# Another order of steps in the first phase and in all periods of a fused attention and feed-forward kernel

## The chip, the cores and the metric

The kernel runs on one core of one Trainium2 chip. The metric is the device time of one execution in microseconds (us); where several executions are shown, their median. All times below are in us unless marked ns. The engines are named as in the profile: PE is TensorE (PEld its weight loads), DVE VectorE, ACT ScalarE, POOL GpSimd and SP SyncE, which here only issues DMAs.

## What is computed

Nyström attention over 8 batches of 8 heads (sequence 576, head size 64, 32 landmarks), and on its result a multiplicative feed-forward layer without a nonlinearity.

```python
q_lm = q.reshape(B, H, m, S // m, D).mean(axis=3)      # 32 landmarks
k_lm = k.reshape(B, H, m, S // m, D).mean(axis=3)
A  = softmax(scale * q @ k_lm.T)
Bm = softmax(scale * q_lm @ k_lm.T)
C  = softmax(scale * q_lm @ k.T)
Z = Bm.T / (norm1(Bm) * norminf(Bm) + 1e-06)
for _ in range(6):
    Z = 2 * Z - Z @ Bm @ Z
x = (A @ Z @ C @ v) as rows of 512                     # 4608 rows
out = ((x @ w1) * (x @ w2)) @ w3 @ w_out               # 512 -> 1024 -> 1024 -> 512
```

Inputs and output are float32; the products run in float16 or float32.

## The kernel before

The kernel is one program whose engines each work through their instructions in the order in which the program issues them; what an engine needs from another it waits for. The order is written out by hand, in five strings of short names (lines 45 to 58 of the profile's line numbers), and `run` issues the steps one after the other. START is issued once, after a fixed beginning that loads weights and starts to fold w3 and w_out into one matrix. Then come eight periods, one for each batch b: FIRST for b = 0, ODD and EVEN in turn for b = 1 to 6, LAST for b = 7. A period b does the attention of batch b+1 up to the matrix g that stands for everything between the normalised A and the feed-forward layer, the first scores C of batch b+2, the two up projections of batch b, and down projections of pairs of batches. START does the whole attention of batch 0 and the scores C of batch 1.

The names, with the engines that each step uses:

- `f`: one product of the fold of w3 and w_out, three PE matmuls of 512 columns; eleven of those in the strings first turn a block of w3 (four PE transposes, one ACT and one DVE copy). `w`: a load of w3 (SP). `x`: turning batch 0's q or k on PE. `v`: batch 0's v (SP).
- `t`: one of four DMA transposes of a batch's q and k (SP). `p`: one of four loads of a batch's v (a tiny ACT copy, then SP). `s`: landmark sums of q or of k, four POOL additions, and between them two POOL-issued loads of the q and k of a later batch. `h`: one of four halves of the landmarks, an ACT copy (tile far) and a POOL addition (tiles qbd for q, lm for k).
- `C0 C1`: scores against all keys (12 PE matmuls each), ACT exponential, three POOL sums (tiles t, es). `S0 S1`: their denominators, two PE matmuls of one column each. `V0 V1`: product with v, 48 small PE matmuls, then an ACT copy into sz.
- `A0 A1`: scores of all queries against the landmarks, PE, then an ACT exponential. `D`: their denominators (PE); `J0 J1 J2` invert them in thirds, `X` splits the result (DVE). `M0 M1`: normalise A (PE, then DVE into ahat).
- `B`, `T`, `N`, `P`, `R`: the landmark matrix Bm (PE, ACT, DVE, POOL), its transpose (DVE, POOL), its norms (DVE), two scaled copies (POOL), the first residual (PE, DVE, POOL).
- `I0` to `I5`: the six steps of the inverse, 16 matmuls of 32x32 each on PE, then a DVE sum (tz) and copy (sz) on which the next step waits. `Z`: closes it (PE, ACT, DVE into zt).
- `G0` to `G3`: zt times w1 and w2, 16 matmuls of 512 columns each, evicted by ACT (even) or DVE (odd) into g.
- `u`: half of a pair of up projections: four PE matmuls; the first of a pair is copied by ACT, the second is multiplied with that copy by DVE. `d` and `db`: half of a down projection, four PE matmuls of 512 columns; the second half ends with an ACT eviction (o_sb) and the output stores on SP. With `d` a new item takes the one bank of tile acc, with `db` one of the three double banks of tile big, which u, I, C, A, G and M share.

On PE most steps use the whole array (u, d, f, C, M, S). A, B, R and G use parts of 64x32, D and V of 128x32, I of 32x32, Z of 128x64; these are called tiled steps, and the shapes tile shapes.

Of the kernel before, what the change touches and what calls it, by code (L numbers as in the profile page):

```python
# [13 lines left out]
B = 8  # L14
H = 8
S = 576
D = 64
# [14 lines left out]
def kernel(  # L32
# [9 lines left out]
    out: bass.AP,  # L42
):
    nc = tc.nc
    START = ("w v x x s f f f f f x x w f f h h s f f w t t f f f f f C0 f f h f h f w t t "
             "S0 C1 B f T f f N V0 f S1 A1 f A0 R D P V1 f J0 I0 p f J1 J2 I1 f f f f f f f "
             "X s I2 p f I3 f f f p I4 f M0 I5 h f s t Z M1 f h f G0 G1 t h f f G2 p h G3 f "
             "f C0 C1 f f t ")
    FIRST = ("u u p S0 u t u B p p u A1 V0 A0 T N u P R u u f s S1 u u D V1 I0 u J1 I1 f J0 "
             "s I2 u h u h J2 I3 u X I4 u u M0 I5 d M1 Z h d t G0 h G1 d p C0 t t G2 C1 G3 "  # L50
             "db ")
    EVEN = ("u S0 u t B u u T V0 A1 u N u u R db u p S1 db A0 V1 p p s u I0 t P D u J0 u I1 "
            "J1 d u I2 db J2 X u I3 u u s I4 M0 I5 h h M1 u Z db h G0 t h G1 db C0 d p G2 t "
            "G3 C1 db ")
    ODD = ("p u S0 t u B A1 p T u p V0 N d R u u S1 s u u d u A0 V1 u I0 D J2 u u I1 J0 d "
           "s I2 P h u u I3 h J1 u u I4 t h d I5 u db X t t d d Z M0 d M1 G0 p G1 C0 d G2 "
           "G3 C1 h db ")
    LAST = ("u u d u u u d u u u d u u u u d u u u u d d db d db db db db db d ")
    consts = ctx.enter_context(tc.tile_pool(name="consts", bufs=1))
    wpool = ctx.enter_context(tc.tile_pool(name="wpool", bufs=1))  # L60
    pin = ctx.enter_context(tc.tile_pool(name="pin", bufs=2))
# [477 lines left out]
    def steps(g, n=1):  # L539
        for _ in range(n):  # L540
            next(g, None)
# [71 lines left out]
    def run(names):  # L613
        for t in names.split():
            if t[0] in queues:
                next(queues[t[0]], None)
            elif t == "f":
                steps(fd)
            elif t[0] == "d":
                piece(acc if t == "d" else lambda: big()[:, 0, :])  # L620
            else:
                n = done[t] = done.get(t, -1) + 1
                while len(atts) <= n and n < B:
                    atts.append(attention(sts[len(atts)]))
                if n < B:
                    atts[n][t[0]](*([int(t[1])] if t[1:] else []))
# [4 lines left out]
    with tc.tile_pool(name="pf", bufs=2) as pf:  # L631
# [50 lines left out]
        steps(fd, 8)  # L682
        run(START)
    pabs = [ctx.enter_context(tc.tile_pool(name="pab0", bufs=1))]
    for b in range(B):
        if b % 2 == 0:
            ab = pabs[b // 2 % len(pabs)].tile([128, 8, 2 * S], FP16, name="ab%d" % (b // 2 % 2))
        sts[b]["ab"], sts[b]["t0"] = ab, S * (b % 2)
        run(FIRST if b == 0 else LAST if b == B - 1 else (EVEN, ODD)[b % 2])
        if b == 0:  # L690
# [32 lines left out]
```

## Time and profile before

| | |
|---|---|
| median of 4 runs | 273.48 us (272.36 to 274.88) |
| the profiled execution: time, span | 272.36 us, 270.6 us |
| granted TensorE clock | 0.998 |
| PE busy | 262.5 us, 97% |
| POOL, DVE, ACT busy | 171.5, 150.6, 143.5 us |
| START begins at (start of its first x) | 18.84 us |
| FIRST begins at (first u) | 67.09 us |
| first ODD, first EVEN, second ODD, second EVEN begin at | 91.92, 118.63, 143.80, 170.18 us |
| last PE work ends at | 266.4 us |

The profile is of one execution. The span goes from its first to its last instruction; the time of the execution has 1.8 us around that. A row of the timeline gives the start and the duration of a group of instructions; on PE the duration holds the time in the pipeline as well, so that the next row begins before the last one ends. What a step costs PE is therefore read from the start of one row to the start of the next.

### The profile page before, as it was taken

The page shows a single profiled execution, that of the slowest core. Times are in us where ns is not written, and L with a number is a line of the kernel's source. Part 1 is how long each engine was busy: PE and PEld are TensorE (multiplying, and loading weights), DVE is VectorE, ACT ScalarE, POOL GpSimd, SP SyncE. Part 2 cuts the span into 40 slices and gives each one's busy share as a digit, 9 for nine tenths or more (in the row PEclk, how much of TensorE's full clock was granted, in tenths as well). Part 3 has the DMA queues.
Part 4 walks back from the last instruction along what each step waited for, and adds up shares of the span by engine and source line. Part 5 has one row for each costly group of instructions (what it writes and reads, how often), then busy time and mean ns, then how long its engine had stood idle before and what let it go on. Part 6 is the DMA issues. An engine that isn't in the chain of part 4 may idle for free.

```text
span 270.6 us, 9335 instructions
## 1 busy us (share of the span) xinstructions
PE 262.5 (97%) x3876; PEld 148.1 (55%) x3876; DVE 150.6 (56%) x380; ACT 143.5 (53%) x276; POOL 171.5 (63%) x237
## 2 busy tenths in 40 slices
PE   8999999999999999999999999999999999999993
PEld 3565555554554565466546654655465556545742
DVE  5643235453567558554866574749466566674420
ACT  4644454246634954385367645844855475435531
POOL 6818971499699879666986994699869545000000
PEclk9999999999999999999999999999999999999999
DMA  6999999999967999998999999989993141113144
GB/s 206 370 241 264 225 249 188 201 219 147 190 137 106 187 184 220 195 186 155 200 168 233 207 169 162 198 131 238 162 257 99 39 125 42 41 42 80 39 111 121
DMA packets 62138, 45.56 MB, mean 168 GB/s; under 512 B 35600, under 2 KB 54288, under 8 KB 62096
## 3 DMA queue, kind: packets, MB, share of 16 engines
q1 hardware_dynamic: 47488, 32.22, 57.0%
q0 software_dynamic: 13824, 11.54, 29.7%
q10 hardware_dynamic: 784, 1.21, 1.4%
q8 instruction: 30, 0.49, 0.8%
q14 instruction: 12, 0.10, 0.1%
HBM read 38.80 MB, written 9.44 MB: 178 GB/s over the span
## 4 chain that ended last, share of the span: by engine, by line
PE 77%; POOL 7%; DMA 5%; SPq 3%; DVE 3%; issue 1%; ACT 1%; DVEq 0%; POOLq 0%
PE big L430 23%; PE acc L471 15%; PE big L471 8%; DMA qkT<-qkn 5%; PE big L379 5%; PE big L413 4%; PE acc L510 4%; PE small L323 4%; SPq L124 3%; PE big L665 2%; PE small L510 2%; DVE ab L436 2%; PE big L230 2%; PE big L497 1%; PE big L364 1%
## 5 line engine op out<-in xcount | busy, mean ns | idle before, releaser
L430 PE MATMUL big<-ahat,gt 128*128 128x288 f16 x512 | 76.1, 286 | 0.4
L436 DVE TENSOR_TENSOR ab<-a_sb,big 128x576 f16<-128x576 f16 x64 | 48.2, 753 | 27.0 <-ACT a_sb L434 15.0
L434 ACT CAST a_sb<-big 128x576 f16<-128x576 f32 x64 | 40.8, 638 | 35.4 <-PE big L430 35.2
L430 PEld LDWEIGHTS <-gt 128*128 128x128 f16 x512 | 46.9, 99 | 19.5
L471 PE MATMUL acc<-w,ab 128*128 128x512 f16 x184 | 47.3, 380 | 0.0
L471 PEld LDWEIGHTS <-ab 128*128 128x128 f16 x280 | 24.3, 99 | 25.9 <-issue 3.2
L510 PE MATMUL acc<-wsp,w3t 128*128 128x512 f16 x144 | 35.4, 380 | 0.0
L194 POOL TENSOR_TENSOR tr<-qkT 128x768 f32<-128x768 f16 x16 | 26.3, 1641 | 7.9 <-DMA qkT<-qkn 7.5
L419 DVE TENSOR_SCALAR gt<-big 128x1024 f16<-128x1024 f32 x16 | 19.6, 1225 | 18.0 <-PE big L413 18.0
L510 PEld LDWEIGHTS <-w3t 128*128 128x128 f16 x192 | 17.9, 98 | 18.0 <-issue 0.8
L195 POOL TENSOR_TENSOR tr<-tr,qkT 128x768 f32<-128x768 f32 x16 | 26.3, 1643 | 1.3
L238 POOL TENSOR_TENSOR t<-ect 96x384 f32<-96x384 f32 x16 | 15.9, 997 | 15.9 <-ACT ect L234 13.8
L471 PE MATMUL big<-w,ab 128*128 128x512 f16 x96 | 23.4, 380 | 0.0
L475 ACT ACTIVATE o_sb<-acc 128x512 f32<-128x512 f32 x23 | 13.7, 596 | 14.0 <-PE acc L471 13.8
L503 DVE SCALAR_TENSOR_TENSOR w3t<-big,w3t 128x512 f16<-128x512 f32 x16 | 11.0, 690 | 18.0 <-ACT w3t L502 18.0
L379 PE MATMUL big<-sz,tz 32*32 32x96 f32 (+1 forms) x768 | 18.9, 248 | 1.1 <-DVE sz L386 0.7
L417 ACT ACTIVATE gt<-big 128x1024 f16<-128x1024 f32 x16 | 16.4, 1023 | 6.3 <-PE big L413 6.3
L384 DVE TENSOR_TENSOR tz<-big,eye 128x64 f32<-128x64 f32 x40 | 8.8, 221 | 15.8 <-PE big L379 15.1
L213 ACT COPY far<-o 64x256 f32<-64x256 f32 x32 | 12.9, 403 | 8.4 <-POOL o L199 7.6
L413 PE MATMUL big<-wup,zt 64*32 64x512 f16 x512 | 17.1, 379 | 0.0
L379 PEld LDWEIGHTS big<-sz,tz 32*32 32x32 f32 x768 | 8.9, 102 | 14.5 <-issue 10.7
L502 ACT ACTIVATE w3t<-big 128x512 f16<-128x512 f32 x16 | 9.5, 596 | 11.0 <-PE big L497 10.9
(104 smaller groups left out, 374.1 us busy)
## 6 DMA issues: line engine op xcount, KB each, us to landing
vt<-in_v_dram SPq DMA_DIRECT2D x28, 288.0 KB, 4.9
out_dram<-o_sb SPq DMA_DIRECT2D x23, 192.0 KB, 2.8
qkn<-in_q_dram POOLq DMA_DIRECT2D x12, 288.0 KB, 5.7
qkn<-in_k_dram POOLq DMA_DIRECT2D x12, 288.0 KB, 6.1
w3f<-in_moe_w_dram SPq DMA_DIRECT2D x6, 512.0 KB, 8.3
out_dram<-o_sb SPq DMA_DIRECT2D x24, 128.0 KB, 2.8
wup<-in_moe_w_dram POOLq DMA_DIRECT2D x4, 512.0 KB, 31.6
out_dram<-o_sb SPq DMA_DIRECT2D x23, 64.0 KB, 2.8
```

Of the source, the lines that this page charges most:

```text
L194: nc.gpsimd.tensor_tensor(out=tr, in0=x[:, :, 0, :], in1=x[:, :, 1, :], op=ALU.add)
L195: nc.gpsimd.tensor_tensor(out=tr, in0=tr, in1=x[:, :, 2, :], op=ALU.add)
L238: nc.gpsimd.tensor_tensor(out=t3[0:NP], in0=e[:, :, 0:3, :], in1=e[:, :, 3:6, :], op=ALU.add)
L379: nc.tensor.matmul(psI[32 * t:32 * t + 32, qd, o:96], tz[sl, qd, :], sz[sl, qd, o:96], start=True, stop=True, tile_position=(32 * h, 32 * t))
L413: nc.tensor.matmul(psG[32 * h:32 * h + 32, qd, :], zt[rs, i, h, :], wup[rs, h, w, fs], start=(i == 0), stop=(i == 1), tile_position=(64 * ...
L417: nc.scalar.activation(out=g[:, :, w, fs], in_=psG, func=AXF.Copy, scale=1.0 / ZS)
L419: nc.vector.tensor_scalar(out=g[:, :, w, fs], in0=psG, scalar1=1.0 / ZS, scalar2=None, op0=ALU.mult)
L430: nc.tensor.matmul(p[:, c, 0:HS], st["g"][:, qd, w, 128 * j:128 * j + 128], st["ahat"][qd][:, c, :], start=(qd == 0), stop=(qd == 1))
L434: nc.scalar.copy(out=st["a_sb"], in_=p[:, :, 0:HS])
L436: nc.vector.tensor_tensor(out=st["ab"][:, j, st["t0"]:st["t0"] + S].rearrange("p (c s) -> p c s", c=2), in0=st["a_sb"], in1=p[:, :, 0:HS], ...
L471: nc.tensor.matmul(pso[:, :], ab[:, j, t0:t0 + 128], w34[:, j, :], start=(j == 0), stop=(j == 7))
L510: nc.tensor.matmul(psW[j][:, :], turned[j, c // 4][:, a, c % 4, :], wsp[:, b, c, :], start=(c == 0 and a + b == 0), stop=(c == 7 and a == 1))
```

## The change

The five strings get another order. No instruction is added or left out, and no function is altered. Counted by name, each string holds what it held before, but for these: one f moves from START to FIRST, START has one t more (8 for 7, so that from FIRST on each period's four t belong to one batch), and one piece in FIRST, EVEN, ODD and LAST is written db for d or d for db. The banks follow from the first half of an item alone: in FIRST, EVEN and ODD they change only for FIRST's first item (big for acc), in LAST for several.

In START, M1 to G3 are taken apart by f, C1 moves behind an f from B, V0 stands ahead of S1, D has R and f between it and A1, I4 and I5 follow each other, I0 follows V1. In FIRST a third u stands ahead of S0, D moves behind I0, M0 behind Z. In EVEN A0 joins R, P moves ahead of the first s, the three p follow V1, J2 stands before I1. In ODD s moves back by a few steps, P and one h ahead of the second s, J1 behind I5, C1 ahead of G2, and the t to later places.

```diff
@@ -42,20 +42,20 @@
     out: bass.AP,
 ):
     nc = tc.nc
-    START = ("w v x x s f f f f f x x w f f h h s f f w t t f f f f f C0 f f h f h f w t t "
-             "S0 C1 B f T f f N V0 f S1 A1 f A0 R D P V1 f J0 I0 p f J1 J2 I1 f f f f f f f "
-             "X s I2 p f I3 f f f p I4 f M0 I5 h f s t Z M1 f h f G0 G1 t h f f G2 p h G3 f "
-             "f C0 C1 f f t ")
-    FIRST = ("u u p S0 u t u B p p u A1 V0 A0 T N u P R u u f s S1 u u D V1 I0 u J1 I1 f J0 "
-             "s I2 u h u h J2 I3 u X I4 u u M0 I5 d M1 Z h d t G0 h G1 d p C0 t t G2 C1 G3 "
-             "db ")
-    EVEN = ("u S0 u t B u u T V0 A1 u N u u R db u p S1 db A0 V1 p p s u I0 t P D u J0 u I1 "
-            "J1 d u I2 db J2 X u I3 u u s I4 M0 I5 h h M1 u Z db h G0 t h G1 db C0 d p G2 t "
-            "G3 C1 db ")
-    ODD = ("p u S0 t u B A1 p T u p V0 N d R u u S1 s u u d u A0 V1 u I0 D J2 u u I1 J0 d "
-           "s I2 P h u u I3 h J1 u u I4 t h d I5 u db X t t d d Z M0 d M1 G0 p G1 C0 d G2 "
-           "G3 C1 h db ")
-    LAST = ("u u d u u u d u u u d u u u u d u u u u d d db d db db db db db d ")
+    START = ("w v x x f f f w f x f s x f h h s f f f f f f f w t f C0 t h f f f w f t f h f "
+             "S0 C1 t f A0 B f T V0 S1 f A1 N R f D V1 P I0 J2 f f f p J0 J1 f I1 f f f I2 f "
+             "f f p p I3 X f I4 I5 f M0 f s h Z f s f f M1 h p G0 t f G1 t h G2 f f f h G3 "
+             "C0 C1 t f t ")
+    FIRST = ("u u p u S0 p u B T p u A0 V0 A1 N u P R u s f S1 u u u V1 I0 u D J1 s I1 J2 h "
+             "u f I2 J0 X u f I3 u I4 u u I5 db M1 Z h d t t h h M0 p G0 G1 d C0 G2 t C1 G3 "
+             "db t ")
+    EVEN = ("u S0 u B u u T V0 A1 N u u R A0 db S1 db u u V1 p p p P s u I0 t D J2 u I1 J0 "
+            "u J1 d u I2 d X u I3 u u s I4 M0 I5 h h M1 u Z db h t G0 h G1 db C0 t p d G2 "
+            "G3 C1 t db ")
+    ODD = ("u S0 u B A1 u p T V0 p N d R p u u u S1 u u d s A0 V1 u I0 D J2 u h u I1 J0 d "
+           "I2 P t t s u u I3 h u u I4 d t h I5 u J1 db X db d Z M0 d M1 G0 G1 C0 p d C1 "
+           "G2 G3 t db h ")
+    LAST = ("u u d u u u d u u u d u u d u u u u u u db db d db db db d d db db ")
     consts = ctx.enter_context(tc.tile_pool(name="consts", bufs=1))
     wpool = ctx.enter_context(tc.tile_pool(name="wpool", bufs=1))
     pin = ctx.enter_context(tc.tile_pool(name="pin", bufs=2))
```

## The prediction

> **What bounds the kernel now.** I read the page first (its busy times and its chain), then the timeline of TensorE alone, start to start, over the whole span, then POOL's, ScalarE's and VectorE's timelines around each wait, then SyncE's queue.
>
> ```profile
> span 270.6 us, 9335 instructions
> ...
> PE 262.5 (97%) x3876; PEld 148.1 (55%) x3876; DVE 150.6 (56%) x380; ACT 143.5 (53%) x276; POOL 171.5 (63%) x237
> ...
> PE 77%; POOL 7%; DMA 5%; SPq 3%; DVE 3%; issue 1%; ACT 1%; DVEq 0%; POOLq 0%
> ```
>
> TensorE is the bound in every stage but the last 4.1 us. Its granted clock is 0.998 of full. A busy share can hide short waits, so I took the time from the start of one step to the start of the next (its slot) and compared all slots of a kind.
>
> ```profile
> 134.73 0.40 PE L379 MATMUL big<-sz,tz 32*32 32x96 f32 x16
> 135.22 0.41 PE L364 MATMUL big<-rmix,selc 128*128 128x144 f16 x4
> 135.87 0.34 PE L379 MATMUL big<-sz,tz 32*32 32x64 f32 x16 [0.23 <-DVE sz L386]
> ...
> 143.80 0.65 PE L430 MATMUL big<-ahat,gt 128*128 128x288 f16 x4
> 144.29 0.28 PE L335 MATMUL small<-ones,es 96*128 96x1 f32 x2
> 144.43 0.65 PE L430 MATMUL big<-ahat,gt 128*128 128x288 f16 x4
> 145.01 0.21 PE L250 MATMUL small<-lm,qbd 64*32 64x32 f16 x5
> ```
>
> The columns are start, duration, engine, line and shapes. The lower four rows: a u takes 0.49 when an untiled step follows (143.80 to 144.29) and 0.58 when a tiled one does (144.43 to 145.01). The same 0.1 is paid on the way out: D takes 0.12 before V, which has the same tile shape, and 0.24 before u. So each change of tile shape costs 0.09 to 0.11. The other slots: d 0.87, f 0.65 (1.09 with its four transposes), V 0.81, I 0.33 (0.27 without the exit), A 0.25, B 0.15, R 0.26, S 0.14, C 0.35, M 0.34, Z 0.37, a pair of G 0.99. The upper three rows are the wait of every EVEN period: I4 to I5 takes 1.14 although only M0 stands between. That is the least time for I to I: product, then the VectorE sum tz (0.23) and copy sz (0.35).
>
> ```profile
> 41.34 0.32 PE L295 MATMUL big<-qkT,lm 64*32 64x288 f16 x8
> 41.64 0.33 PE L309 MATMUL small<-bt,btm 64*32 64x32 f32 x16
> 42.43 0.31 PE L343 MATMUL small<-eat,onesq 128*32 128x144 f16 x8 [0.47 <-ACT eat L301]
> ...
> 68.81 0.38 PE L335 MATMUL small<-ones,es 96*128 96x1 f32 x2 [0.58 <-POOL es L243]
> ...
> 76.02 0.85 PE L323 MATMUL small<-vt,ect 96*32 96x64 f32 x48
> 76.79 0.35 PE L379 MATMUL big<-sz,tz 32*32 32x96 f32 x2
> 77.31 0.39 PE L379 MATMUL big<-sz,tz 32*32 32x96 f32 x14 [0.17 <-ACT sz L327]
> ```
>
> These are the waits of START and FIRST: D waits 0.53 for the exponential of A0 (A to D takes 1.09 at least), S0 waits 0.58 for POOL, and I0 straight after V1 costs 1.29 for both, 0.48 more than V's slot. All excess of slots over their usual value is about 4.6 us: START 1.1; FIRST 1.5; EVEN 0.5 in each of 3; ODD 0.17 in each of 3. That is the most that any order of the same work can give back, besides shape changes.
>
> ```profile
> 66.70 0.99 POOL L238 TENSOR_TENSOR t<-ect 96x384 f32<-96x384 f32 x1
> 67.78 0.45 POOL L241 TENSOR_TENSOR es<-t 96x128 f32<-96x128 f32 x1
> 68.31 0.45 POOL L243 TENSOR_TENSOR es<-es,t 96x128 f32<-96x128 f32 x1
> ```
>
> S0 hangs on C0 through ScalarE's exponential and these three POOL sums: 31.74 (C0) to 33.17 (first sum) is 1.43, the sums take 2.06, the hand-over 0.05, so C to S is 3.54 at least.
>
> **Shape changes.** Counted over the strings (START + FIRST + 3 EVEN + 3 ODD): before 27+29+3x29+3x28 = 227, after 25+30+3x28+3x28 = 223. Four fewer at 0.1 give -0.4, of which -0.3 is in EVEN, where R and A0 now stand together. [...]
>
> **START.** Step by step against the old order:
> - S1 comes earlier after C1. TensorE's work between is C 0.35, f 0.75, A0 0.14, B 0.16, f 0.74, V0 0.81 = 2.95 against 3.54: +0.6 (before, 35.53 to 40.13 was 4.60, no wait).
> - D now has R and f between it and A1 (over 1.09): -0.53.
> - V1 then I0 with no f between: +0.48, by FIRST's rows.
> - I3 f I4: 0.33+0.74 = 1.07 against 1.14: +0.07. I4 I5 with nothing between: 1.14-0.27 = +0.87.
> - Two shape changes fewer: -0.2.
>
> Sum +1.3 before C0. The sums and copies around Z hold nobody up: s comes no earlier on POOL, since POOL waited 7.45 there for the transposes' DMA (51.16), and the h now ahead of Z needs o, ready at 56.7, while Z stays near 58. So C0 moves from 65.08 to 66.4, and S0 from 68.81 to 66.4+3.54 = 69.9: +1.1. One f is moved to FIRST (+0.65) and one u ahead of S0 (-0.49), which only trade places.
>
> **FIRST.** B then has one u less ahead of it: 69.9+0.14+0.59 = 70.65, against 70.13, so +0.5. POOL's chain from there (bm, btm, tz, two s, four h) starts +0.5 later, its old idle 0.75 ahead of bm being the cover that takes the other half. Waits after R: before 0.48 (V1 I0), 0.22 (I0 u I1), 0.22 (I3 u I4), 0.3 (M0), 0.06 = 1.3; after 0.48, then I0 u D I1 1.14 = none, I3 u I4 0.23 and another 0.3 because J0 (0.46) and X (0.30+0.36) now sit on VectorE ahead of I3's sum: 1.0. One shape change more: +0.1. TensorE then reaches ODD's S0 +0.3 late, POOL's sums +0.4 to +0.5 (they set S0 already, with 0.22 of wait at 92.63). I take **+0.5** for START and FIRST together. Bounds: -1.3 if the new waits are covered and half of the 2.6 goes, +1.5 if START's +1.3 is kept.
>
> **EVEN and ODD.** EVEN's steps on TensorE are the same multiset; -0.1 from R A0. I0 D u I1 is 0.33+0.24+0.58 = 1.15, just the chain's 1.14; J2 (0.46) and u's product (0.75) follow the sum on VectorE, and I2 is 2.3 away, so 0 (bound +0.3). The old 0.5 at I4 M0 I5 stays: nothing around it moved. P (0.31+0.72) passes ahead of s on POOL, behind which the same total follows. In ODD TensorE's order changes only in one u around S1 and d, and C1 ahead of G2: 0 (bounds -0.17 to +0.3). On POOL, P and one qbd of h (0.74) pass ahead of the second s, which ends 1.85 later, 110.9 for 109.07; its two loads (0.69 each to issue, 6.1 to land) are late by as much, with transposes that are used some 14 us on. Each t (1.5 to 2.3 on SyncE's queue) that waits for such a load holds the output stores behind it; before it did so too (stores at 110.03 and 116.25), and three o_sb buffers cover 2.8 of landing. p costs ScalarE 0.19 and SyncE 0.3 wherever it stands; V is a period later. Three EVEN: **-0.3**.
>
> **LAST.** Six u in a row: the fifth needs the buffer that the first pair's product frees. In the old run from 252.83 the cast starts at 253.52 and the product ends at 254.96, 2.13 after the start; the fifth u wants it at 4x0.49 = 1.96: +0.2. The later banks (acc and big in turn) are free, and the final 4.1 us keep their order. **+0.2** (bounds 0 to +0.5).
>
> Sum: +0.5-0.3+0.2 = +0.4. The profiled execution took 272.36 (span 270.6 and 1.8 around it), the fastest of four; on it 272.8. On the median, 273.48, it makes 273.9. The 1.1 between the two is spread that the profile does not explain.
>
> **Rivals.**
> - Slower: ScalarE is held by a far copy. In ODD the third h waits for the second s. It now has d's eviction ahead and zt (112.73) behind, on which G0 waits. By the rows far ends at 111.3. If POOL's second s ends beyond 112.3, 1.4 later than I reckon, each us more delays zt, G0, C0 and the next S0, whose margin is 0.19 (es ready 118.93, S0 119.12). At 1 us over, three ODD give +3.0: 276.9. For it: POOL works without a pause from 97.06 to 113.1, and already made this copy wait 0.86. Against: 1.4 of room, and POOL idles 3.77 after. This side also holds an ODD or EVEN wait that is three times 0.7 by another chain. Chance 0.30.
> - Faster: START's new waits do not arise (POOL free at S1, an overlap at I5) and those of START and FIRST go entirely, 2.6, with EVEN's 0.3: 270.6. Against: V1 I0 and I4 I5 have nothing to cover them. Chance 0.08.
> - It does not do what it says: the runs stay as dense (223 against 227 changes of shape) and only neighbours swap. Then -0.4 plus waits, which is my forecast: 0.62.
>
> **How the numbers follow.** A measurement of this kernel can tell about 1%, 2.7 us, from no change. The forecast's own range is 272.2 (-1.3) to 275.3 (+1.5 and 0.3). The slower rival's price carries the range to 277.2; beyond it and below lies under 0.2. Faster by over 1% 0.08, within 0.62, slower 0.30.
>
> **What would show it.** START: I5 0.87 after I4's own slot, S1 waiting for POOL's es, D not waiting. FIRST: S0 near 69.9, ODD's S0 near 93. EVEN periods 25.1 and ODD 26.4 long (25.17 and 26.38 before), R to A0 0.16. LAST: a wait of 0.2 in the run of six u. I am wrong if an ODD or EVEN period moves by more than 0.4, if C0 comes before 66, or if a slot of V, I or A itself changes with its neighbours by more than 0.1.

## The result, and the profile after

| | before | after |
|---|---|---|
| median of all runs | 273.32 us (271.89 to 278.08, 53 runs) | 275.5 us (272.95 to 281.37, 32 runs) |
| ratio after to before | | 1.0051 [1.0029, 1.0073] |
| profiled execution: time, span | 272.36, 270.6 | 276.96, 275.2 |
| its granted TensorE clock | 0.998 | 0.994 |

The ratio makes +1.4 us of 273.3, a small loss that the measurement can tell from nothing but that stays within 1%. The ratio leaves out executions that took over 1.5% more than the fastest of their kernel, 9 of the 32 of after and, by the same rule, 4 of the 53 of before; eight of those nine had a clock of 0.985 to 0.994, which a stop like the one that this section ends on may have caused, so the ratio is rather too small. The medians of all runs differ by 2.2 us, and the spread is 8.4 us for 6.2.

The page of after, the lines that answer to those of before, with the rows of TensorE's busy share and granted clock in 40 slices of the span:

```profile
span 275.2 us, 9344 instructions
...
PE 263.8 (96%) x3876; PEld 148.2 (54%) x3876; DVE 152.5 (55%) x380; ACT 143.5 (52%) x276; POOL 171.5 (62%) x237
...
PE   8999999999999999999999999799999999999993
...
PEclk9999999999999999999999999799999999999999
...
PE 85%; DMA 4%; DVE 3%; ACT 3%; issue 1%; POOL 1%; SPq 0%; ACTq 0%; DVEq 0%; POOLq 0%
```

The work is the same. The 26th slice, from 172 to 179, is the odd one: TensorE is idle there and its clock falls. The span is 4.6 longer. To see where, I took both kernels' times from each S0 to the next:

| stretch | before | after | difference |
|---|---|---|---|
| span's start to the first ODD's S0 | 92.63 | 93.22 | +0.59 |
| first ODD to S0 of the first EVEN | 26.49 | 26.48 | -0.01 |
| first EVEN | 25.17 | 25.57 | +0.40 |
| second ODD | 26.38 | 26.46 | +0.08 |
| second EVEN | 25.30 | 28.56 | +3.26 |
| third ODD | 26.38 | 26.38 | 0 |
| third EVEN and LAST, to the last product | 42.17 | 42.42 | +0.25 |

The +0.40 of the first EVEN is a small case of what follows: an output eviction at 119.81 waits 0.64 for a store, the copy behind it is late, and TensorE waits 0.30 for that copy at 121.55.

TensorE's timeline of after in START, the rows that answer to the forecast's waits:

```profile
40.43 0.35 PE L335 MATMUL small<-ones,es 96*128 96x1 f32 x2 [0.53 <-ACT sz L327]
...
42.64 0.84 PE L323 MATMUL small<-vt,ect 96*32 96x64 f32 x48
...
43.93 0.39 PE L379 MATMUL big<-sz,tz 32*32 32x96 f32 x14 [0.17 <-ACT sz L327]
...
54.59 0.40 PE L379 MATMUL big<-sz,tz 32*32 32x96 f32 x16
55.72 0.34 PE L379 MATMUL big<-sz,tz 32*32 32x64 f32 x16 [0.73 <-DVE sz L386]
...
69.75 0.38 PE L335 MATMUL small<-ones,es 96*128 96x1 f32 x2 [0.57 <-POOL es L243]
```

V1 to I0 takes 1.29 and I4 to I5 1.13; S0 waits for POOL and starts at 69.75. All three had been forecast (1.29, 1.14, 69.9). S1, in the first row, waits 0.53, but for ScalarE's copy sz of V0 and not for POOL's sum es, which was ready at 39.99.

TensorE's timeline of after at the start of the second EVEN period:

```profile
171.24 0.65 PE L430 MATMUL big<-ahat,gt 128*128 128x288 f16 x4
...
172.60 0.66 PE L430 MATMUL big<-ahat,gt 128*128 128x288 f16 x4
175.15 0.65 PE L430 MATMUL big<-ahat,gt 128*128 128x288 f16 x4 [1.88 <-ACT a_sb L434]
...
177.27 2.10 PE L430 MATMUL big<-ahat,gt 128*128 128x288 f16 x8
```

A u at 175.15 waits 1.88 for the ScalarE copy (a_sb) that empties its bank. Two u, 1.08 elsewhere, then take 2.03 (177.27 to the next row at 179.30). Why the copy is late, from ScalarE's timeline:

```profile
170.19 1.01 ACT L417 ACTIVATE gt<-big 128x1024 f16<-128x1024 f32 x1
173.41 0.60 ACT L475 ACTIVATE o_sb<-acc 128x512 f32<-128x512 f32 x1 [2.21 <-DMA out_dram<-o_sb]
174.03 0.40 ACT L213 COPY far<-o 64x256 f32<-64x256 f32 x1
174.46 0.64 ACT L434 CAST a_sb<-big 128x576 f16<-128x576 f32 x1
```

An output eviction stands ahead of the cast and waits 2.21 until a store has left its o_sb buffer. There are three buffers, and the evictions before it began at 161.51, 164.10 and 166.55: it needs the buffer of 161.51. SyncE's queue says when that store was issued, in after and then in before (issue times; two stores for each eviction):

```profile
155.09 1.48 SPq L480 DMA_DIRECT2D out_dram<-o_sb  x2
161.55 5.24 SPq L124 DMA_TRANSPOSE qkT<-qkn  x2
166.88 1.34 SPq L480 DMA_DIRECT2D out_dram<-o_sb  x2
168.32 2.19 SPq L124 DMA_TRANSPOSE qkT<-qkn  x1
170.60 2.52 SPq L480 DMA_DIRECT2D out_dram<-o_sb  x4
```

```profile
157.37 1.98 SPq L124 DMA_TRANSPOSE qkT<-qkn  x1
161.66 0.79 SPq L480 DMA_DIRECT2D out_dram<-o_sb  x2
162.54 5.48 SPq L124 DMA_TRANSPOSE qkT<-qkn  x2
```

In before the eviction at 161.05 ends at 161.65 and its stores go at 161.66, ahead of two transposes (t). In after it ends at 162.11 and its stores go at 166.88, behind two t that SyncE could begin only at 161.55, with its queue standing from 156.57: 4.8 us in the queue. The t had waited 4.9 for the load of q, whose pieces took 8.4 to land in this execution and 5.5 in before (medians of those issued from 150 to 160). The landing comes on top: the buffer came free 6.5 after the issue (166.88 to 173.41); the page's median for stores of 192 KB is 4.6, in before 2.8. In before the eviction due at that place, at 170.82, needs the buffer whose stores went at 161.66.

What the stop leads to, in stretches of 2 us (columns: stretch, length, busy time of PE, its weight loads, VectorE, ScalarE and POOL with the number of instructions, then the granted clock, the DMA engines' busy share, GB/s):

```profile
174.00:176.00 2.00, 0.85 (x24) 0.56 (x26) 0.87 (x2) 1.71 (x5) 0.72 (x1) 1.00 1.04 345
176.00:178.00 2.00, 2.00 (x56) 1.32 (x45) 1.83 (x8) 0.91 (x2) 0.69 (x2) 0.52 1.03 255
178.00:180.00 2.00, 2.00 (x32) 1.01 (x31) 0.72 (x3) 0.80 (x3) 0.00 (x0) 0.62 0.04 9
```

The clock is 0.52 and 0.62 for the two stretches behind the gap: of the 3.26, 1.88 is the wait and some 1.4 the slow work after it.

A wait for a store need not cost anything. ScalarE's timeline of before has one too:

```profile
214.73 0.60 ACT L475 ACTIVATE o_sb<-big 128x512 f32<-128x512 f32 x1 [2.00 <-DMA out_dram<-o_sb]
```

TensorE does not stop there, and the period, the third ODD, takes its usual 26.38.

### The profile page after: what moved, and what is told of

It is laid out like the page before. It is cut to its first block, busy times and chain, and to the rows that moved or that the text cites. A ratio compares the mean times of both kernels' runs of the same rounds, so it can differ in the third digit from the quotient of the medians.

```text
span 275.2 us, 9344 instructions
## 1 busy us (share of the span) xinstructions
PE 263.8 (96%) x3876; PEld 148.2 (54%) x3876; DVE 152.5 (55%) x380; ACT 143.5 (52%) x276; POOL 171.5 (62%) x237
## 4 chain that ended last, share of the span: by engine, by line
PE 85%; DMA 4%; DVE 3%; ACT 3%; issue 1%; POOL 1%; SPq 0%; ACTq 0%; DVEq 0%; POOLq 0%
PE big L430 22%; PE acc L471 14%; PE acc L510 11%; PE big L471 8%; PE big L379 5%; PE small L323 5%; PE big L413 5%; PE small L510 4%; PE big L497 2%; DMA out_dram<-o_sb 2%; DMA wof<-in_moe_w_out_dram 2%; PE big L230 2%; PE big L295 1%; PE big L364 1%; DVE ab L436 1%
## 5 line engine op out<-in xcount | busy, mean ns | idle before, releaser
L430 PE MATMUL big<-ahat,gt 128*128 128x288 f16 x512 | 77.9, 289 | 2.5 <-ACT a_sb L434 2.2
L510 PE MATMUL acc<-wsp,w3t 128*128 128x512 f16 x144 | 36.1, 379 | 0.5 <-DVE wsp L491 0.3
L502 ACT ACTIVATE w3t<-big 128x512 f16<-128x512 f32 x16 | 9.5, 596 | 11.9 <-PE big L497 11.8
```

Of the source, the lines that this page charges most:

```text
L430: nc.tensor.matmul(p[:, c, 0:HS], st["g"][:, qd, w, 128 * j:128 * j + 128], st["ahat"][qd][:, c, :], start=(qd == 0), stop=(qd == 1))
L510: nc.tensor.matmul(psW[j][:, :], turned[j, c // 4][:, a, c % 4, :], wsp[:, b, c, :], start=(c == 0 and a + b == 0), stop=(c == 7 and a == 1))
```

## The experiments

**Theory 1**: the order of ODD makes the stores late; an eviction then waits for its o_sb buffer, holds ScalarE, and TensorE stops in some executions more, in others less. **Rivals**: the loss is START's waits, which the trace prices at 0.6 to 1.0; or another order inside the periods, independent of the stores. A fourth o_sb buffer separates them, but it also takes memory, which came from a tile of TensorE's warm-up (512 columns cut to 16); so before got the same in e5.

**e1: after with a fourth o_sb buffer**

```diff
-            o_sb = po.tile([128, DM], FP32, name="o_sb")
+            o_sb = po.tile([128, DM], FP32, name="o_sb", bufs=4)
...
-        warm = pf.tile([128, 512], FP16, name="warm", bufs=1)
+        warm = pf.tile([128, 16], FP16, name="warm", bufs=1)
```

> The changed kernel with four o_sb buffers instead of three (the scratch tile warm is cut to 16 columns to make room). Theory 1, stores: in ODD the output stores stand on SyncE behind transposes that wait for their loads, an o_sb buffer comes free late, ScalarE waits for it (2.2 us at 171 in the changed kernel's profile), u of the next EVEN waits for ScalarE, and TensorE's clock drops after that. A fourth buffer takes the wait away: no ScalarE wait for a store, no u waiting over 0.2, clock 1.00 throughout, 273.3 to 274.0 with a narrow spread, ratio 1.001 to 1.003. Theory 2, START, FIRST and LAST: the loss is the 0.6 + 0.2 of their new waits and the rest of the first trace is chance: ratio stays near 1.005.

Measured: 273.27 (272.84 to 274.38, 12 runs), ratio 0.9986 [0.9964, 1.0008]. The loss is gone. The spread is 1.5 us for 8.4, but 5.8 in e5 and 6.3 in e4, so it proves little by itself. ScalarE's timeline of e1 at the same place:

```profile
171.25 0.60 ACT L475 ACTIVATE o_sb<-acc 128x512 f32<-128x512 f32 x1 [0.24 <-PE acc L471]
...
172.30 0.64 ACT L434 CAST a_sb<-big 128x576 f16<-128x576 f32 x1
```

The eviction waits for its matmuls alone, and the cast comes 2.2 earlier. No wait for a store is left in its whole profile, and its periods are 25.17 and 26.38, those of before. In this execution the stores of the eviction at 161.32 also left earlier, at 163.17; that the buffer matters is shown by the times, less by this trace.

**e5: before with a fourth o_sb buffer** (the same two lines, in before)

> The kernel before with four o_sb buffers. Theory 1, stores (the changed order makes ScalarE wait for o_sb where TensorE feels it, the old order seldom does): at most a little faster, ratio 0.996 to 1.000, by the executions of before that hold such a wait (2.0 us at 214 in its profile). Theory 2, any kernel gains from the fourth buffer as much as the changed one did (1.0051 to 0.9986, 0.65%): ratio 0.994 or below.

Measured: 273.26 (271.90 to 277.69, 12 runs), ratio 0.9998 [0.9972, 1.0024]. Before gains nothing from the buffer that takes the whole loss from after, and neither does the cut tile matter. So the loss belongs to the new order and hangs on the number of o_sb buffers: by the trace of after, on the stores that free them.

**e9 and e11: two o_sb buffers, in after and in before**

```diff
-            o_sb = po.tile([128, DM], FP32, name="o_sb")
+            o_sb = po.tile([128, DM], FP32, name="o_sb", bufs=2)
```

> The changed kernel with two o_sb buffers instead of three. Theory 1, stores: the wait of ScalarE for a store's landing comes in every ODD and longer, TensorE waits for u at the EVEN starts and elsewhere: +3 to +15 us, ratio 1.015 to 1.06, and more than the same cut costs the kernel before. Theory 2, the fourth buffer gained by chance or by its place in memory: under 1.01.

> The kernel before with two o_sb buffers. Theory 1: slower too, but clearly less than the changed kernel with two, since its stores leave earlier: ratio 1.005 to 1.03. Theory 2: under 1.01, like the other.

Measured: after 285.72 (284.27 to 287.17, 4 runs), ratio 1.0460 [1.0413, 1.0507]; before 276.45 (275.28 to 279.80, 4 runs), ratio 1.0107 [1.0062, 1.0152]. By 2, 3 and 4 buffers, after stands at 1.046, 1.0051 and 0.9986 and before at 1.0107, 1 and 0.9998: each buffer less costs the new order more than the old. ScalarE's timeline of e9:

```profile
123.33 0.60 ACT L475 ACTIVATE o_sb<-acc 128x512 f32<-128x512 f32 x1 [9.75 <-DMA out_dram<-o_sb]
```

One eviction waits 9.75 at the end of the first ODD; a t holds SyncE's queue there for 3.59 (from 116.64). ScalarE loses 14.5 us to such waits in all (9.4 in e11), and TensorE stops for 7.80; its clock from 118 to 126 is 0.52.

**e3: the old START in after** (the old string of START with one more t at its end; FIRST without its last f, which is START's again)

```diff
-    START = ("w v x x f f f w f x f s x f h h s f f f f f f f w t f C0 t h f f f w f t f h f "
...
-             "C0 C1 t f t ")
+    START = ("w v x x s f f f f f x x w f f h h s f f w t t f f f f f C0 f f h f h f w t t "
...
+             "f C0 C1 f f t t ")
...
-             "u f I2 J0 X u f I3 u I4 u u I5 db M1 Z h d t t h h M0 p G0 G1 d C0 G2 t C1 G3 "
-             "db t ")
+             "u f I2 J0 X u I3 u I4 u u I5 db M1 Z h d t t h h M0 p G0 G1 d C0 G2 t C1 G3 db "
+             "t ")
```

> The changed kernel with START in the old order (one t appended, and FIRST without its last f, so that the sum of steps is kept). Theory 1: START is worth 0.6 at FIRST's end at most; the EVEN starts still wait for the stores in some executions: ratio 1.003 to 1.005. Theory 2: the ratio falls to 1.001 or below, and S0 of FIRST is near 68.8.

Measured: 275.18 (272.63 to 277.69, 12 runs), ratio 1.0047 [1.0014, 1.0080]. The loss stays; its profile has four waits for stores, 4.1 us, and a stop of TensorE of 0.96 at 172.93, at the start of the second EVEN as in after. START is not the cause.

**e4: the old ODD in after** (with its first t moved to its end, as the loads now need)

```diff
-    ODD = ("u S0 u B A1 u p T V0 p N d R p u u u S1 u u d s A0 V1 u I0 D J2 u h u I1 J0 d "
-           "I2 P t t s u u I3 h u u I4 d t h I5 u J1 db X db d Z M0 d M1 G0 G1 C0 p d C1 "
-           "G2 G3 t db h ")
+    ODD = ("p u S0 u B A1 p T u p V0 N d R u u S1 s u u d u A0 V1 u I0 D J2 u u I1 J0 d s "
+           "I2 P h u u I3 h J1 u u I4 t h d I5 u db X t t d d Z M0 d M1 G0 p G1 C0 d G2 G3 "
+           "C1 h db t ")
```

> The changed kernel with ODD in the old order (its first t stands at its end instead, since START now holds that one). Theory 1: the sums of k are early again, the transposes wait less and the stores behind them leave earlier: ratio 1.001 to 1.003, no wait for o_sb over 0.5. Theory 2: ratio near 1.005, since TensorE's order in ODD is nearly the same in both.

Measured: 273.45 (273.01 to 279.26, 13 runs), ratio 0.9992 [0.9964, 1.0019]. With three buffers and the old ODD the loss is gone. Its profiled execution (279.21) lost its time in START, where TensorE waits 2.44 at 41.70 for a load of w3; the f that follows takes 1.42 (42.58 to 44.00), a later one 0.74 (46.02 to 46.76). Its first EVEN takes 25.83, with a stop of 0.42 that no semaphore explains; the later periods are the usual ones. The expectation of no wait for o_sb over 0.5 was missed: there is one of 2.00 at 221.30, which, like that of before, does not stop TensorE. Three more runs undo one part of ODD at a time.

**e2: ODD's t behind the neighbouring stores**

```diff
-           "I2 P t t s u u I3 h u u I4 d t h I5 u J1 db X db d Z M0 d M1 G0 G1 C0 p d C1 "
-           "G2 G3 t db h ")
+           "I2 P s u u I3 h u u I4 d t t h I5 u J1 db X db t d Z M0 d M1 G0 G1 C0 p d C1 "
+           "G2 G3 db t h ")
```

> The changed kernel with ODD's four transposes moved behind the output stores next to them; the order on TensorE, ScalarE, VectorE and GpSimd is the same, only SyncE's queue differs. Theory 1: the stores leave early, the wait for o_sb is gone, ratio 1.001 to 1.003. Theory 2: 1.005. If the transposes then come too late for the sums of the next period, GpSimd shows a wait for qkT.

Measured: 274.67 (273.55 to 277.12, 12 runs), ratio 1.0051 [1.0021, 1.0081]. The loss stays. The wait at 171 is gone from its profile, but evictions wait at 152.20 (0.67) and 217.61 (1.51) instead: the stores behind these t were helped, others not. Neither wait costs TensorE anything. What this profile loses, 2.3 in the second EVEN (27.57 for 25.30), it loses in two stops of TensorE that no semaphore explains (the last section), so that e2's loss comes through the stores is not shown.

**e7: POOL's old order in ODD** (the second s ahead of P, the first h back behind P)

```diff
-    ODD = ("u S0 u B A1 u p T V0 p N d R p u u u S1 u u d s A0 V1 u I0 D J2 u h u I1 J0 d "
-           "I2 P t t s u u I3 h u u I4 d t h I5 u J1 db X db d Z M0 d M1 G0 G1 C0 p d C1 "
+    ODD = ("u S0 u B A1 u p T V0 p N d R p u u u S1 u u d s A0 V1 u I0 D J2 u u I1 J0 d s "
+           "I2 P h t t u u I3 h u u I4 d t h I5 u J1 db X db d Z M0 d M1 G0 G1 C0 p d C1 "
```

> The changed kernel with only GpSimd's order in ODD as before: the second s stands ahead of P and of the first h again, t and p stay. Theory 1a, the sums of k end 1.85 late, their loads too, and the transposes and stores behind them: the wait for o_sb goes, ratio 0.999 to 1.001. Theory 1b, the loads of v, issued later, take DMA time from the loads of q, whose transposes then hold the store: ratio stays near 1.005.

Measured: 274.08 (273.12 to 283.69, 12 runs), ratio 1.0037 [1.0006, 1.0068]; two waits of 0.67 for stores in the profiled execution. The interval reaches from nearly no loss to all of it, so a part of the cause may lie here; it is no cure.

**e8: ODD's loads of v (p) at their old places**

```diff
-    ODD = ("u S0 u B A1 u p T V0 p N d R p u u u S1 u u d s A0 V1 u I0 D J2 u h u I1 J0 d "
-           "I2 P t t s u u I3 h u u I4 d t h I5 u J1 db X db d Z M0 d M1 G0 G1 C0 p d C1 "
+    ODD = ("p u S0 u B A1 p T u p V0 N d R u u u S1 u u d s A0 V1 u I0 D J2 u h u I1 J0 d "
+           "I2 P t t s u u I3 h u u I4 d t h I5 u J1 db X db d Z M0 d M1 G0 p G1 C0 d C1 "
```

> The changed kernel with only ODD's four p at their old places (three at its beginning, the fourth after G0). Theory 1b: the loads of q land 5 us after their issue again and not 8, the transposes leave early, ratio 0.999 to 1.001. Theory 1a: near 1.005.

Measured: 276.00 (273.17 to 278.49, 12 runs), ratio 1.0048 [1.0008, 1.0087]; one wait of 1.49 for a store in the profiled execution. No cure, and this execution, the fastest of the twelve, does not show where the others lose: the wait does not stop TensorE.

So without ODD's new order the loss does not come, and none of its three parts that I undid alone clearly undoes it. Which combination makes the stores late is open, and so is whether ODD's order alone, in the kernel before, would do it.

**e6: four buffers, the old START and the old LAST** (e1's edit, e3's START and FIRST, and before's LAST)

```diff
...
-    LAST = ("u u d u u u d u u u d u u d u u u u u u db db d db db db d d db db ")
+    LAST = ("u u d u u u d u u u d u u u u d u u u u d d db d db db db db db d ")
...
```

> The changed kernel with four o_sb buffers, START in the old order (one t appended, FIRST without its last f) and LAST in the old order; so FIRST, EVEN and ODD are new. With the wait for the stores gone this prices the terms of START and LAST. If the prediction's terms hold (about +0.7 by the trace of the changed kernel at ODD's first S0, and +0.2 for the run of six u), the ratio is 0.9986 - 0.0033 = 0.995; if START's waits cost nothing in the end it stays at 0.9986.

Measured: 272.89 (271.44 to 274.10, 12 runs), ratio 0.9982 [0.9954, 1.0010]. In the traces, from START's first x to the first ODD's S0 takes 73.79 in before, 74.5 in e1 and 73.52 here: the new START costs 1.0, the new FIRST gives 0.3 back. From the third EVEN's S0 to the last product takes 42.17, 42.37 and 42.15: the new LAST costs 0.2. These are single executions. The times do not show the 1.2: they would have gone from 0.9986 to 0.994, and the expected 0.995 was missed. Why is open.

**e10: four buffers, the old LAST, three f moved into START's waits**

```diff
-             "S0 C1 t f A0 B f T V0 S1 f A1 N R f D V1 P I0 J2 f f f p J0 J1 f I1 f f f I2 f "
-             "f f p p I3 X f I4 I5 f M0 f s h Z f s f f M1 h p G0 t f G1 t h G2 f f f h G3 "
+             "S0 C1 t f A0 B f T V0 f S1 A1 N R f D V1 P f I0 J2 f f p J0 J1 f I1 f f f I2 f "
+             "f f p p I3 X f I4 f I5 M0 f s h Z f s f f M1 h p G0 t f G1 t h G2 f f f h G3 "
...
```

> The changed kernel with four o_sb buffers, LAST in the old order, and three f of START moved by one place, so that f stands between V0 and S1, between P and I0, and between I4 and I5. If START's waits are what the prediction said (0.53, 0.48 and 0.87), they go, C0 comes 1 earlier, near 65, S0 near 68.8, and the trace is 1.0 shorter than with the four buffers alone (0.8 in START, 0.2 in LAST): ratio 0.9986 - 0.0035 = 0.995. If START's waits are covered later the ratio stays at 0.9986.

Measured: 272.82 (271.54 to 275.88, 12 runs), ratio 0.9979 [0.9945, 1.0012]. The shorter START is not in its trace: S0 is at 70.77, later than after's 69.75, with a wait of 1.29 for a load of w3 at 39.71. Of the other profiled executions only e4's has such a wait in START; both have the new START, and whether its order makes that load late more often is not tested.

**e12: e10 with e4's ODD**

> The same with ODD in the old order as well (its first t at its end). Theory 1: with four buffers the order of ODD no longer matters, 0.993 to 0.997, within 0.2% of the kernel with the new ODD. Theory 2, ODD's order costs something besides the stores: at least 0.3% faster than that.

Measured: 272.41 (271.45 to 276.25, 12 runs), ratio 0.9984 [0.9955, 1.0013]. Beside e10 (0.9979) no difference between the two orders of ODD can be seen once there are four buffers, as Theory 1 has it; the intervals would hide one of 0.4%. Its gain against before stays short of what was expected: C0 waits 1.49 at 67.12 for a POOL sum (qbd), and S0 is at 70.84. Covering START's waits does not bring C0 forward where POOL's landmarks set it. No version here can be told from before: every interval of the best three, e6, e10 and e12, holds 1.

## Why the prediction was right where it was, and the step that failed

The measured median, 275.5, lies in the range, and +1.4 by the ratio is within 1%, as forecast. But the +0.4 summed what TensorE's own order costs; most of what was measured comes from a term that it put at nothing. The median lies above 275.3, where the forecast's own bounds end; the range held it because the price of a rival that did not come, 3.0 for a late far copy, had carried it to 277.2. That part is luck.

- **START and FIRST, +0.5**: measured +0.59 at the first ODD's S0, +0.73 counted from the first x. C0 is at 66.13 (forecast 66.4), S0 at 69.75 (69.9), ODD's S0 at 93.22 ("near 93"). D no longer waits. S1 waits 0.53 (0.6), but the reason given was wrong: it should have waited for POOL's sums, 3.54 behind C1, and these were ready 0.4 before it began. It waits for the copy out of V0's product, which now stands directly ahead of it; that the sizes agree is chance.
- **EVEN, -0.3**: did not come; a period without a stop takes 25.17 in e1, as the first one does in before. R and A0 joined take 0.38, where apart they took 0.27 and 0.25, so the gain is there, but S1, now behind db, takes 0.22 instead of 0.14, and the period as a whole is no shorter. The count of shape changes took a step's own slot as fixed; it was not, though both neighbours here use the whole array.
- **LAST, +0.2**: right (six u take 3.14 instead of 2.94, and e6 has it back).
- **ODD, 0: the step that failed.** "Each t (1.5 to 2.3 on SyncE's queue) that waits for such a load holds the output stores behind it; before it did so too (stores at 110.03 and 116.25), and three o_sb buffers cover 2.8 of landing." It named the mechanism and cleared it with the landing alone. What must be covered is the time in the queue and the landing: in after 4.8 in the queue behind two t, and a median landing of 4.6. The eviction that was due at 171.20 (2.21 before 173.41) needs the buffer of 161.51, 9.7 us later; 0.6 for the eviction, 4.8 in the queue and 6.5 until the buffer came free make 11.9. By e1, e5, e9 and e11 this term is worth the whole loss: 1.0051 with three buffers, 0.9986 with four, some 1.8 us.
- **The slower rival** put the danger in ScalarE, held in ODD by a far copy that waits for POOL, at 3.0. ScalarE was held, at ODD's end, but by an eviction that waits for a store. That one stop cost 3.26, close to the 3.0, is chance: it came once in the profiled execution, not three times, and 1.4 of it was the clock.
- **"I am wrong if an ODD or EVEN period moves by more than 0.4"**: the second EVEN did, by 3.26, and that line pointed at the fault.

Without the stores' term the forecast would be measured by e1 against e5: 0.9986 / 0.9998 = 0.9988, and from the two intervals about 0.0034 to either side. The +0.4 (1.0015) lies within that, but so does no change. In the traces, from the first x to the start of the last product, before takes 245.68 and e1 246.47: +0.8, with 0.7 in START and FIRST, 0.2 in LAST, and 0 and -0.1 in the first two EVEN. Why the ratio makes 1.4 while the profiled execution lost 4.6 is argued, not shown: a buffer may come free too late in some executions and in time in others. The profiled executions of e7 and e8 took 273.2, 0.8 and 2.8 below their medians, and no wait for a store stops TensorE in them.

## What to carry to other kernels

When steps that issue DMAs are moved, ask of each queue not only when the moved DMA starts, but what is issued behind it and which buffer that gives back; the slack to compare is buffers times the spacing of the evictions, against time in the queue plus landing (here 9.7 against 4.8 and 6.5, with 0.6 for the eviction itself). A short run with one buffer more and one with one fewer, in both kernels, tells in four numbers whether such a wait is the cause. A single profile shows just one draw of such a wait: those of after and e3 have a stop from it (1.88 and 0.96), those of e2, e7 and e8 do not.

## What the runs showed of the hardware

**Behind a stop of 1.88 the granted clock was 0.52.** In after the stop ends at 175.15, and TensorE ran at 0.52 and 0.62 in the two stretches of 2 us from 176 to 180, and at 1.00 from 180 to 182. Behind longer stops the work is slow as well. In e9, with a stop of 7.80, the clock is 0.52 from 118 to 126, and 32 matmuls of G behind it take 1.84 (126.44 to 128.28), where ahead of it they took 1.01 (114.66 to 115.67). In e11, behind 3.87, they take 1.84 (120.20 to 122.04) for 1.01, and in e4, behind 2.44, an f takes 1.42 for 0.74. Behind three shorter stops it is not: in e2, with one of 1.05, the clock is 1.00 in every stretch from 170 to 184; in e3, behind 0.96, two u take 1.09 (174.56 to 175.65); in e10, behind 1.29, an f takes 0.74 (40.18 to 40.92). An estimate from the trace of after: at a clock of 1.00 the stop would have cost its own 1.88 and not 3.26.

**TensorE stops without a semaphore.** TensorE's timeline of e2, one V cut in two:

```profile
173.37 0.54 PE L323 MATMUL small<-vt,ect 96*32 96x64 f32 x24
174.96 0.54 PE L323 MATMUL small<-vt,ect 96*32 96x64 f32 x24 [1.05 <-issue]
```

The profile shows nothing that it waited for. The next such stop (0.80) ends at 181.84 and cuts a V in two as well. What held TensorE was not shown. The DMA engines were less busy around the two stops than shortly before: their busy share was 0.97 from 174 to 176 and 0.44 from 180 to 182, where it was 1.79 from 170 to 172. Smaller stops of this kind stand in e4 (0.42), e5 (0.21), e10 (0.27 and 0.53) and e11 (0.60 and 0.21), so also in the old order.
